# Sharing the first and last 32 score columns of five query tiles, written by matmuls in 32x64 tiles of the array

## The chip, the cores and the metric

The kernel runs on one core of one Trainium2 chip. The metric is the device time of one execution in microseconds (us), and a kernel's time is the median of its runs. Besides the timed runs there is one profiled execution, from which every busy time, start and duration below is taken. The engines are TensorE (PE, with its weight loads as PEld), VectorE (DVE), ScalarE (ACT), GpSimd (POOL) and SyncE (SP, which issues most DMAs).

## The reference

The input x has 2048 rows of 512. Four layers are added to it one after another, each on the layer norm of what stands before it: linear attention (A), attention in a sliding window (B), and both once more with the same weights. There are 32 heads of 16 columns.

```python
def _B_ref(x, wqkv, wo):
    H = 32; Dh = D // H; W = 256
    ...
    scores = jnp.einsum("bhqd,bhkd->bhqk", q, k) * (Dh ** -0.5)
    idx = jnp.arange(S)
    mask = (idx[:, None] - idx[None, :] >= 0) & (idx[:, None] - idx[None, :] < W)
    scores = jnp.where(mask[None, None], scores, -1e9)
    p = _softmax(scores, axis=-1)
    o = jnp.einsum("bhqk,bhkd->bhqd", p, v)
    ...
x = x + _A_ref(_layernorm(x), A_wqkv, A_wo)
x = x + _B_ref(_layernorm(x), B_wqkv, B_wo)
x = x + _A_ref(_layernorm(x), A_wqkv, A_wo)
x = x + _B_ref(_layernorm(x), B_wqkv, B_wo)
```

A query sees itself and the 255 rows before it. Turned round, a key at row n is seen by the queries n to n + 255, and a block of 64 keys by 320 queries.

## The kernel before, in words

The rows are cut into 16 tiles of 128 (j = 0 to 15; the title of the change counts from one, so its tiles ten to fourteen are j = 9 to 13). The layers overlap: `middle(2)` runs the second layer (window) tile by tile, with the keys of the third layer behind it; `middle(3)` runs the last layer (window), with the outputs of the third ahead of it. For each tile, `middle` calls `front` three tiles ahead (`a_out`: the third layer's output product; `norm`: layer norm and transpose to xT; `b_qkv`: the queries into XQ, the keys by way of a DMA into kB), `b_v` one tile ahead, then the scores, the values and the output product of the tile itself.

**Scores.** kB holds keys so that one weight load of 32 rows serves two heads: 32 rows are two heads of 16 columns, and the 128 columns of the weights are 64 keys times two heads, laid out key by key (block diagonal by a DMA that writes zeros between). Four row groups of the array (gq, 32 rows each) work on four pairs of heads at once, each into a PSUM bank of its own. So the scores stand transposed: 128 partitions are 64 keys times two heads, and the free side is the queries. Partitions 0 to 63 are the first 32 keys of the block, 64 to 127 the last 32.

`b_scores` (matmuls L634, exps L644, masks L652) writes, for one half-tile b of 64 keys and two of the four groups f, the first 256 of the block's 320 query columns: 8 matmuls of 256 columns, two exps on ACT of 1024 elements per partition (two banks each) into the buffer of probabilities P, and on DVE one mask of the first 64 columns (upper triangle). There are four such bursts to a tile, so eight exps. `b_far` (L723, L732) writes the last 64 columns of all of a tile's blocks at once: 32 matmuls of 64 columns and two exps of 1024, into columns 256 to 319 of P; `far_masks` (L703 on POOL or L704 on DVE) zeroes the lower triangle there. The far columns are read by the values of tile j + 2, the others by those of j to j + 2. P is a ring of four slots in the last layer, three in the buffer pb and one in vp; tiles 3, 7, 11 and 15 use vp.

`b_values` (L753) multiplies P by the values, 24 matmuls of 34 columns for a group f; the 34 columns hold two heads' 16 values and a one for the sum; DVE divides (L765, L766). `b_out` transposes by DMA (L371), multiplies by wo (L400) and adds (L568).

**Packed tiles.** `middle` holds a second form for tiles named in PACK: before `b_scores` it calls `b_edge`, and in place of `b_far` only `far_masks`. In `b_scores` the window then begins 32 queries later (sh = 32): it covers columns 32 to 287, and its mask has 32 columns in place of 64. The two strips that are left, columns 0 to 31 and 288 to 319, each matter for one half of the partitions only: no query of the first strip sees the last 32 keys of its block, and no query of the last strip sees the first 32. `b_edge` puts both in one strip: partitions 0 to 63 hold the first strip's scores, 64 to 127 the last one's. Two exps of 512 elements write it to columns 288 to 319 of P, and a DVE operation named `ma` copies partitions 0 to 63 from there, times the triangle, to columns 0 to 31. Then `far_masks` zeroes what must be zero at 256 to 319. The values of tile j read what `ma` writes. Partitions 64 to 127 of columns 0 to 31 keep the zeros that the mask of the slot's earlier tile left. PACK is empty in this kernel, so no tile takes this form.

**Order.** Nothing is scheduled at run time. `Plan` builds a list of operations with their dependencies and a key; `place` reads from TABLE (a compressed string) one order of all operations, the engine of each operation that has a choice, and a PSUM bank for each tile of PSUM. Each engine runs its operations in that order, and `synchronise` adds the semaphore waits. The costs given with each operation (`occ`, `act`, `dve`) belong to the planner and have no effect on the running program.

Of the kernel before, what the change touches and what calls it, by code (L numbers as in the profile page):

```python
# [217 lines left out]
PACK = {}  # L218
# [5 lines left out]
def bass_view(x, free):  # L224

    return bass.AP(x.tensor, x.offset, [x.ap[0]] + free)


class Plan:
# [430 lines left out]
    def b_edge(self, j, key):  # L660
# [224 lines left out]
    r"q*|$7s?a*Wo~3T8S1PT(rNZdAdWFiZPN~}}oerXQtJ5mI-lf87)baEk6;9t(XH*7Fy0I#tU#pC|pk_T=WzuKW9Cc3_{YJ&tqKByjx`2AChN~v3rY@-7sS)bF",
    r"s-;J&@cO+fq$B9kYLxn@N~nlBvo5TQ=t%m5imbEfggUEsDv{2ntxl}7>nJ*jE~=C2LaLZ{y0}iJE2|PZs!py;>Iy1{4z5b+e5$rCtb(bEx{l7N>*?XTk}j>A",
    r">&m){uA)|{7P_jgrbp=Nx`uA4SF5_Zl4_;bsHVD|ZmgT>J*u2)qZ{fby1s6$%d5Srfj+0!sz$o4KCddOeQKm$r$*`h>VlfBtE<s^j=rc4=`p&b`lPC=HF~U`",
    r"s}JjO`m>s+$Lj}bf_|tDsEK;MKBC*}NqT`^t1qdAdYWFOzo_YYonEXTsmZ#7e&c57y?TmXuV?Cxx|9B@rs`RGgWjh*>y7%d-mkmp<$9BTtXAmFdWn9bw&<05",
    r"ss5&}=w-UA4gy#8QGG)Pg=_kj?xu^uDt$~BhhT71AJ+%;6CFgK&`<SAy;YZhQ+k_zrh~%{9aJCG+x2t3Q<sEb`nrChcj?tSD!kOuAOr;0r644n)*<vOeMX0Z",
    r"(hwT%=;&}(hk<jthPtQE>xb@wzN@?IG7t}X=!^OkB!JVfN0)`_@LI=*a&QJ>K@GUAW5WoD2{mCP#DV*|HY9_D@J7GYF(5fS(C_p^Jqj-A6gmZ@)Q|LT9T&>O",  # L890
    r"d!0%@)~TQZeATISY8VY+Asmc>G>}G*g$NKHB0@zN2X$aPoP|U%0qQ~}hy;nD9-M=ox)!v6^N<88LsDo37hon_gjtXhT0&a*rY}Ji_^xL|1NfoSK_f^HKlN>B",
    r"2(96R&HxJP!ySkW8b0ZaFcI!Tc9;YJA9Wj;440uDTmgi}Ku|`1(QTouz6zNj3Y62Ibq>e^)gUJ{fvS)TGDB0C2hAWG<c2A*0H#8D&5#G?Lj|1|3^a#mS|A@R",
    r"ghh}QrolB>4A&t)SSSGPA-cW+OP~Wd=m;_NQdk9@Af{dhYhVt<(#v5kbcWT?ORs>Quo8Ofb+7^Y>4H!Q`s(!%2K(r+xE2b-6W9o^-7_cxn;;x+hNAEk!s7?1",
    r"h#%oORKhK=6?(xZsEoVe0Yt#wPz4`CM9ii8z<tQABjF?H3teCu&VZ_zM@Pon*bg2<6zm3Zu|MS1(=ng!3IiY>R>OgC2WQ|Qh>z9r4b;Fr&>h~wUbqK$u?O_m",
    r"@1Q2`gKaQCZ-*B!9bUp`*a5fTJ?w{McoV)r3OoR>;42)2*RTtc<4jD1QE{M7g5Mw-?u73!7@{L$VjKeLa3~ytx|k5tV+<Syvv4@X#MzhuQ(`8ZgGsR-X2w)l",
    r"A5&u%jD^kdFtos|SPPFpMy!o#uqCF&)>sD#+aO~ryocGaEgJj**)a~z#h=g!6JQQ(j5$%EU}roEO|T0tN5E!y47#Gm6__8pqs8OU4qv#H*dBZ0JiL!5paVX@",
    r"lh6YluEE&Y5er}t?1byEAojwC_|gT%ZnzeM;Rbw!y|EB(#6Gwln_^*n<u>7C%!Ng;FD}BO*bj5#V%&@ku^7(B;+O}Q;0`Q-3vd^{!G-u1^WjcxfP-{!9IS_6",
    r"UVMikaF~AULgF4AqE}-A+KZvEBo5W3a36-ogw!8P<4|0R1F#GZ!$h<SpWr|&i_7pSCZ;3!47cELJc?U!HzuJGcnp)$S8Ph#a6cxa@7Rn+Vsd(p%_#*9#&7rn",
    r"4`2&=iKFl%wxl0;5I^H~9F41J5FWx$xS9^*7(~iQt!OMVWun%UlG+f_8v1~#C=GqV%ybeB39Y5nbR5%?rJwj7(~+WA=;#EtrEH|>6awX-(>M;Z(-|C(K`0kZ",
    r"z_S>Xa??Z%M(1!6p2s|tlZsJRx`4syJ%ymxSb{##I?78OX+2%U;`EU&VIkT;ou~-qqmq<`I#YfsOyQ_E6`*!hkor(jYEPx8FLj{)^odH-0P07Vu?!8QD_E93",  # L900
    r"Q%KrKS1|((qVN=oBG5IgOxLj+g{JNlk#^H2ibOqVG=-%-G?pUMWK2(cX$nT6F;tGCQWg3_(WnAdrRWrfwox^jirc9?^`zmngTB&W>PjQ2It`&NG>%5lX8J}$",
    r"={p^u8dQmD(iS>I!zc!ArCt=1YSBSDLbYiW)u9`Blq%9q98b6K7)_v9bb%()aWZ_7CXw(A(tL?51IMN_beZbXSvpMh2zei!pmP+5_R~qKPv<EppQ0-ij89Vo",
    r"x=IZxIEQ4%*JvhPr%)V%XVG2yL9;0|N8}*<ljcw)&cbs^aaNv3k$E!Br$)4s7SI%GOxbuB-J>Qnl@`){ipmctE=A*M6pvc)LyFEf=n=K#=|p^s9@8U^Pt1?`",
    r"Cbi-xbeI=W7=FS}DK5w0BOH&P@@)#sQ8+#?rlTB=pYamP%i%dD=jRB#lw$ER%Evi5JKv$@l#8EHY+gYH_!zIG+<b;}@L4X(=lDDq=Qw<U^Kc?A#uvFHALr6s",
# [36 lines left out]
class Kernel(Plan):  # L941
# [152 lines left out]
```

## Time and profile before

| | |
|---|---|
| Median of 3 runs | 416.91 us (416.87 to 417.95) |
| The profiled execution | 415.97 us |
| Its span | 414.2 us |
| Mean granted clock of TensorE | 0.999 |
| Busy: PE, DVE, ACT, POOL | 387.9, 346.8, 345.8, 117.7 us |
| Weight loads (beside PE) | 258.5 us |
| Exps of the wide scores, L644, both window layers | 224, 206.7 us |
| Exps of the far columns, L732, with 1024 elements, into pb | 50, 49.6 us |
| Share of the chain that ended last | PE 48%, ACT 35%, DVE 9%, DMA 5% |

A busy time counts the time in which an engine has an instruction in flight; two that overlap count once. The mean duration of one instruction is therefore longer than busy time over count where instructions follow each other closely. "<-" names what ended an engine's idle time. The chain of work that ended last is followed back from the last instruction, at each step to what released it. Numbers behind an L are lines of the kernel before.

### The profile page before, as it was taken

How to read it: one execution, taken by the hardware profiler on the slowest of the kernel's cores; microseconds unless marked ns; L12 is line 12 of the kernel's file. 1: busy time of each engine (PE TensorE's matmuls, PEld its weight loads, DVE VectorE, ACT ScalarE, POOL GpSimd, SP SyncE). 2: the span in 40 equal slices, each digit the busy share in tenths (PEclk: the TensorE clock that was granted, in tenths of full speed). 3: DMA queues.
4: the chain of work that ended last, by engine and by line, in shares of the span. 5: the costliest groups of instructions: out<-in, count | busy, mean ns of one | idle time of the engine just before them, and what ended most of it. 6: DMA issues, size and time to landing. Idle time of an engine off the chain costs nothing.

```text
span 414.2 us, 17130 instructions
## 1 busy us (share of the span) xinstructions
PE 387.9 (94%) x7481; PEld 258.5 (62%) x7555; DVE 346.8 (84%) x803; ACT 345.8 (83%) x432; POOL 117.7 (28%) x211
## 2 busy tenths in 40 slices
PE   7999999999999999999999999999999989988886
PEld 3545676766575577565666777586757745556554
DVE  5997898989989988778978689989799687776575
ACT  2624449998999999999997245999999999999992
POOL 4784833111241243230112302220132215230111
PEclk9999999999999999999999999999999999999999
DMA  7545316632233624444213100353306623273361
GB/s 246 177 79 148 104 40 119 131 92 68 64 96 78 110 73 113 80 107 106 56 29 69 26 2 27 93 148 79 81 7 134 137 56 95 60 159 96 93 121 54
DMA packets 67555, 37.83 MB, mean 91 GB/s; under 512 B 48248, under 2 KB 62584, under 8 KB 67480
## 3 DMA queue, kind: packets, MB, share of 16 engines
q1 hardware_dynamic: 67040, 35.54, 36.7%
q8 instruction: 60, 0.98, 1.0%
q0 software_dynamic: 432, 1.18, 0.9%
q14 instruction: 15, 0.12, 0.1%
q10 hardware_dynamic: 8, 0.00, 0.0%
HBM read 6.29 MB, written 2.10 MB: 20 GB/s over the span
## 4 chain that ended last, share of the span: by engine, by line
PE 48%; ACT 35%; DVE 9%; DMA 5%; issue 2%; SPq 1%
ACT pb L644 22%; PE ps L400 17%; PE ps L414 13%; PE ps L753 7%; ACT pb L732 6%; ACT vp L644 5%; PE ps L634 5%; PE ps L475 2%; DMA XQ<-xn 2%; DVE stats L361 2%; DMA xres<-in_A_x_dram 2%; DVE xres L568 1%; DVE XQ L557 1%; PE ps L723 1%; ACT vp L732 1%
## 5 line engine op out<-in xcount | busy, mean ns | idle before, releaser
L644 ACT ACTIVATE pb<-ps 128x1024 bf16<-128x1024 f32 (+2 forms) x224 | 206.7, 1042 | 4.5 <-PE ps L634 3.7
L753 PEld LDWEIGHTS ps<-vB,pb 128*128 128x128 bf16 x2560 | 77.5, 96 | 11.7 <-issue 4.6
L753 PE MATMUL ps<-vB,pb 128*128 128x34 bf16 x2560 | 83.2, 177 | 1.1 <-ACT pb L644 0.6
L414 PE MATMUL ps<-xT,wBp 128*128 128x128 bf16 x1024 | 69.2, 219 | 1.2 <-DVE vp L586 0.5
L414 PEld LDWEIGHTS ps<-xT,wBp 128*128 128x128 bf16 x1024 | 59.2, 98 | 13.6 <-issue 4.4
L423 ACT ACTIVATE tE<-ps 128x512 bf16<-128x512 f32 x64 | 38.5, 612 | 34.3 <-PE ps L400 15.5
L363 POOL TENSOR_SCALAR ve<-mv 128x1 f32<-128x1 f32 x64 | 16.7, 261 | 172.6 <-DVE mv L362 170.5
L634 PE MATMUL ps<-XQ,kB 32*128 32x256 bf16 (+2 forms) x1024 | 49.6, 267 | 5.0 <-ACT vp L644 1.4
L732 ACT ACTIVATE pb<-ps 128x1024 bf16<-128x1024 f32 x50 | 49.6, 1066 | 0.4 <-PE ps L723 0.2
L568 DVE TENSOR_TENSOR xres<-ps,xres 128x512 bf16<-128x512 f32 x63 | 43.1, 685 | 7.6 <-PE ps L400 7.0
L400 PE MATMUL ps<-wA,XQ 128*128 128x512 bf16 x176 | 46.2, 379 | 2.7 <-issue 0.6
L652 DVE TENSOR_TENSOR pb<-pb,tri 128x512 bf16<-128x512 bf16 x112 | 44.7, 412 | 4.0 <-ACT pb L644 3.7
L703 POOL TENSOR_SCALAR_AFFINE_SELECT pb<-pb 128x1024 bf16<-128x1024 bf16 x26 | 29.8, 1148 | 62.9 <-DVE pb L652 32.6
L361 DVE BATCH_NORM_STATS2 stats<-xres 128x6 f32<-128x512 bf16 x64 | 43.6, 686 | 2.6 <-DMA xres<-in_A_x_dram 1.8
L364 POOL TENSOR_TENSOR rs<-ve,negh 128x1 f32<-128x1 f32 x64 | 37.8, 591 | 5.3
L634 PEld LDWEIGHTS ps<-XQ,kB 32*128 32x128 bf16 x1024 | 15.5, 92 | 33.6 <-ACT pb L644 9.2
L414 PE MATMUL ps<-XQ,wA 128*128 128x128 bf16 x512 | 34.7, 219 | 0.3 <-DVE o L766 0.3
L414 PEld LDWEIGHTS ps<-XQ,wA 128*128 128x128 bf16 x512 | 30.4, 98 | 5.7 <-DVE o L766 0.6
L400 PE MATMUL ps<-wBv,xT 128*128 128x512 bf16 x112 | 31.5, 380 | 2.2 <-issue 1.3
L400 PE MATMUL ps<-wBo,oT 128*128 128x512 bf16 x105 | 28.8, 380 | 4.2 <-issue 1.1
L400 PE MATMUL ps<-M,XQ 128*128 128x512 bf16 x112 | 30.7, 380 | 2.1 <-issue 1.0
L765 DVE RECIPROCAL rc<-ps 128x16 f32<-128x16 f32 x64 | 16.1, 252 | 19.3 <-PE ps L753 19.0
(110 smaller groups left out, 532.8 us busy)
## 6 DMA issues: line engine op xcount, KB each, us to landing
vB<-vS SPq DMA_DIRECT2D x64, 136.0 KB, 2.6
kB<-vp SPq DMA_DIRECT2D x64, 128.0 KB, 2.7
wA<-in_A_wqkv_dram SPq DMA_DIRECT2D x3, 512.0 KB, 4.6
out_dram<-xres POOLq DMA_DIRECT2D x9, 128.0 KB, 2.8
xres<-in_A_x_dram SPq DMA_DIRECT2D x2, 512.0 KB, 4.3
pb<-in_B_wqkv_dram SPq DMA_DIRECT2D x1, 1024.0 KB, 5.6
xres<-in_A_x_dram SPq DMA_DIRECT2D x3, 256.0 KB, 4.8
out_dram<-xres SPq DMA_DIRECT2D x6, 128.0 KB, 2.4
```

The costliest lines, as they stand in the source:

```text
L361: self.on("DVE", "stats", lambda e: e.bn_stats(K.stats[:, t, :], K.xres[:, t, :]), key, dve(512), rd=[("xres", t)], wr=[("stats", t)])
L364: self.pow = self.on("POOL", "pow", lambda e: e.tensor_tensor(K.rs[:, t, :], K.ve[:, t, :], K.negh[:], ALU.pow), key + 0.03, (640, 690), r ...
L400: m = e.matmul(K.ps(ps), lhs(c), rhs(c), start=c == 0, stop=c == 3)
L414: m = e.matmul(K.ps(ps)[:, f * P:(f + 1) * P], w(c, f), xT(c), start=c == 0, stop=c == 3)
L423: self.on("ACT", "E", lambda e: e.activation(K.tE[:, s, :], K.ps(ps), ACT.Exp, bias=0.0), key, act(512), wr=[("tE", s)], ps=[ps])
L568: self.on("DVE", "res", lambda e: e.tensor_tensor(K.xres[:, t, :], K.ps(po), K.xres[:, t, :], ALU.add), key, dve(512), rd=[("xres", t)], w ...
L634: m = e.matmul(K.ps(ps[gq])[:, ns * i:ns * i + ns], K.kB[rows, j % 4, 2 * f + b, :, :], K.XQ[rows, f, q:q + ns], start=True, stop=True, ti ...
L644: return e.activation(out(2 * h, 2, ns), i, ACT.Exp, bias=0.0, scale=0.25)
L652: return e.tensor_tensor(x, x, K.tri[:, 0, sh:64].unsqueeze(1).unsqueeze(1).to_broadcast([P, 4, n, 64 - sh]), ALU.mult)
L703: return e.affine_select(out=x, in_=x, compare_op=ALU.is_ge, fill=0.0, base=-2, pattern=[[0, 16], [-2, 64]], channel_multiplier=1)
L732: return e.activation(far(h), i, ACT.Exp, bias=0.0, scale=0.25)
L753: m = e.matmul(K.ps(ps)[:, 34 * u:34 * u + 34], K.P((b // 2) % rp)[:, gq, f, o:o + P], K.vB[:, (b // 2) % 4, b % 2, r, :], start=i == 0, s ...
```

## The change

PACK names tiles 9 to 13 of the last layer (phase 3). `b_edge` is rewritten: each matmul of 128 weight columns and 2 x 32 queries becomes two of 64 weight columns and 32 queries, at array positions of 32 rows by 64 columns. Half u = 0 takes the first 32 keys with the first strip's queries and writes partitions 0 to 63; u = 1 takes the last 32 keys with the last strip's queries (288 further on) and writes partitions 64 to 127 of the same PSUM columns. The two DVE copies (`gc`) that the old form of `b_edge` needed to bring the strips together are gone, and the exps read 32 columns in a row where they read 32 of every 64. TABLE is replaced as a whole, since the list of operations is another.

```diff
-PACK = {}
+PACK = {3: (9, 10, 11, 12, 13, )}
...
             for f in range(4):
                 for b in range(2):
-                    q = P * j + 64 * b
                     for gq in range(4):
                         rows = slice(32 * gq, 32 * gq + 32)
-                        c = 128 * f + 64 * b
-                        m = e.matmul(K.ps(ps[gq])[:, c:c + 64], K.kB[rows, j % 4, 2 * f + b, :, :], bass_view(K.XQ[rows, f, q:q + 32], [[288, 2], [1, 32]]), start=True, stop=True, tile_position=(32 * gq, 0))
+                        c = 64 * f + 32 * b
+                        for u in range(2):
+                            q = P * j + 64 * b + 288 * u
+                            half = slice(64 * u, 64 * u + 64)
+                            m = e.matmul(K.PS[half, ps[gq].banks[0], c:c + 32], K.kB[rows, j % 4, 2 * f + b, 32 * u:32 * u + 32, :], K.XQ[rows, f, q:q + 32], start=True, stop=True, tile_position=(32 * gq, 64 * u))
             return m
 
-        self.pe("s", put, key, 1, 512, mode=(32, 128), occ=245, rd=[("kB", j % 4, 0), ("kB", j % 4, 1), ("XQ", j), ("XQ", j + 2)], ps=ps)
+        self.pe("s", put, key, 1, 256, mode=(32, 64), occ=540, rd=[("kB", j % 4, 0), ("kB", j % 4, 1), ("XQ", j), ("XQ", j + 2)], ps=ps)
...
-            side = lambda c, two=two: bass_view(K.PS[64:128, two[0].banks[0], c:c + 32], [[512 * (two[1].banks[0] - two[0].banks[0]), 2], [64, 8], [1, 32]])
-            self.on("DVE", "gc", lambda e, side=side: e.tensor_copy(side(0), side(32)), key, dve(512), ps=two)
 
             def ex(e, h=h, two=two):
-                return e.activation(edge(h), K.pair(two, [[128, 4], [64, 2], [1, 32]]), ACT.Exp, bias=0.0, scale=0.25)
+                return e.activation(edge(h), K.pair(two, [[64, 4], [32, 2], [1, 32]]), ACT.Exp, bias=0.0, scale=0.25)
...
 TABLE = (
...
 )
```

More of the change, by code (lines that the diff above doesn't have):

```diff
@@ L885 @@
[L885 to L892, printed above, removed]
@@ new lines @@
+    r")71&(R0!CiPO2FyBwSai;f4wYITS%$xT#93nMy-wxTQ|1FmPM#RHs!MXs8$(sd(^G<x{Vef$A_zy;ix@U6mHzs5?ratf~QT)etpQ<%M(*7K*6cDj$S{^pGDi",
+    r"z<U)Q-l+mGOqEmxAwEQaoT?C5hzNO90vN6wj8F+7h>8S>AR`1)iJ_8;44I&cDh!#S2xNhpP!zI4ew7rGKrzS;1ypg!1|^}qss)vx1Qb+tpdvJd@=yU*sH&<N",
+    r"RE8>06)LN0&>U8(+E84zfK{rDY78x*AvA$qYPD(&b)gYdP-j#<SflF0SyfIofHtsOol~t~I1Gh7Y6KjBy=o-Pgjp~O4#I4>r#`6BuuqMFRWJwctFiD=jf3-Q",
+    r"Jj{hdFb~?o1h}A9!vi%RroaODq}ISxSO~*lBD8~Pup1`9ba<%R!&>M7lVJwzfld%qEroUPNG*f)a1pw|a@YWiU?c2>#n2Hp!6jG%ogoljhQm+<_rW#ztggTj",
@@ new lines @@
+    r"_@V;i4LAx#aX$pXV-N_g!&NATk03BSf#VPqH^T|o0>v>1Y=g%T47b7x*bc!lG6sc}Py%<rO$dR{AQ+UyDEJ(9!AS^-r7$Xn!c*`9Zoz3d19#vhoQ0>*6>h^h",
+    r"h=bkW0-V5jcoKI)X{?HI@f4Q97<d<|VN4u`)iD|l$5?n8&qES?1tTyzzJ_F&4C3QGcmv5HDZYiW7#m08eMkW*@Bx&=lz0Xo!dVQBDd97O!BkL9rNVF+7Q<tC",
+    r"9EG*;97e#=SOIHe4NQPzuqGzNu~-MsV>29w$+03P!WNhqr(<fIft9d1et`=(6Td<|{029%0p7yzkOu2xT}+F&@g1bY@%RDK;{<GoSyACdd=C>5uoYfH#5PD+",
+    r"3N&8E($E?|LI%u+pCA%u#OzoZ8(}8QfmN_E=ER6t2IgQEY=V<;E;hx<SQauPV>y_I26N#Qi~@qWaRGJ*i&t<F=E1fY74l+B%!gNTAv$b_^YI$C$Hf>8R$vEQ",
@@ new lines @@
+    r"f*o-c&cf)h6k|YlT#4`9GVB4%@tx}lvvCdfhIN=93*c&8i@hKe^?}e-5Fg=sEQC*R0~W@O7=|9>I}A(Z={;7UO&E?gV-E~ZAFv|r#CsTlo?=hDkCi9~^uj6h",
+    r"0CPe_>W!T+66J!M^bkAaRO*Adp)ba!JkSN>P(PeTx2Q73rB~P=yW#-cg|Bfp-llHY7vA6=oQ7NQBi_JgScSIYTkHpS@HtkcZ8#N^&|dt6$*3BA#(nq#tJ8jb",
+    r"iAiZYCZOpQneJjDnn6+M3(lm0cpalsLVDw7QG6PN$>}Smp?EYH6H{$UOGHC38V$uASclS428vD@DFq$C7?hGSQC(_Esi+1W#AcM54q;8oOq$YDbE-uxiK!K}",
+    r"pe$slHGM;&tn?i%H6TaXs3B!1MS*BG<)x0)hz?_Cx<g9|C>9;TyVQx=&@zfi_Xw#gHKC*U+AXL1)Rwx_96E;W=s0$xRrG-JQG0qwYp4h1rw-JGR?|A_4}qyC",
@@ new lines @@
+    r"6`&xro_bM1`rtOuT53!=s5dR3Lez)qQBEpM3uz;*pt)3p7EvzRM)RmB6{8*Wit^BWdQIDD0IZ~-l$!>^8yZBxXb`-0!D$x_fp~fk)u#{?Uk`@jw3|Xw2}+>*",
+    r"Qb`(2{iqZ@qJ;V}^{3J_gc9jPG?WtSO>~%^P!heF_R<mBNuOy8HP%V>S8AdMQZoINw$c|mO3$dN-bagR7(J)=)J*TEkJMbR(C_E~4W|#ZQXixd^pd_2=~X(F",
+    r"9!X0`>lXSLrPjwOxn@0zK2dtTTBpzhXfzouI;GB_t^Q7LX^qaP*J`DmPNQ4uEE@C)YNfMj)UEYN3Z%zSR(*=b(hE9GIrKORtaIu!G@gR!vowKn>2<n@4yv>3",
+    r"w>p?UN5%9zeV*Fu-1-8&*F|*)T|jr#d2}XSNPp0Ib!J^$7t~>NPyJEn)1P!3onQCTg>_r~S(ni5bZ^~Pm(>0AMJlB)QGZ=p_tC-idL33@rgXZC4ymtDMIBCG",
@@ new lines @@
+    r"rLH=J4zG9W4SJW3pu6eNdZdo1C(>>`TBp^MXn^jaBk4+dl%7o8br~I5SJvfp6x~U0(V=t|9aV4DWp!0OR1eg{b!S~oZ`0NFApJ!T(>3%yJy>tlL-YZ?N!Qf1",
+    r"bTnOFZ`S*DbUi{J(qHv88lw;EgZesE&|~!xeS^m782X&vqsME*6ZCm~R0~hjz!$V-<e2)DCO)Rm=vaEMuB|WX)4Gm6uIuWvIxwHmmvj(5sq5*>y1ov|!TE}w",
+    r"uCMA49E@k^+xnZHsY7yj4#eN}EFFO}vE$iVab}*QBl1K&S2xf*^gKODH`G~pyS}3v>B)M&zN;hiJsn#|;i)<l$I;C=Dqqw0b#rFEt|RdSexNnC;DbCx-_Q>^",
+    r"u3n%Y@k1S(AM+uO!;kbW9hwhwTwbW3a2Srpi*#;|&Wm+k4$I*<1~1Whc&X0HG5N91&awE3UZ!(!K0d|Eb$mX;IXN2_=F^;ji*hbL%V+qeKF3A4IG^XET$1zi",
@@ new lines @@
+    r"F)qL*I3Bm>f?SNBatAKO&$tkG<kp;!+i)T-&55}!m*FJ*oO^RwE<=5|6Ti~sxE=T9vQ&j%@N4~&%TafJqg!!j?!ig9AGhQ#oQ!+&Ois>Ebqao_XK`0f$-Q_s",
+    r"ALnlTT$kq;x<6OoIs8(e;EG(82k=R*%u{(FzvAgUh^z559?a>v5?AM?{GOL_4PMT#xh5~<6<muy@M5098F&%b<{|usm+(;j$aOdsXXLuPl0We<Ud6+CF0bZ!",
+    r"yoMX|d>+B6`7JNtk=%sS@LC?l7q}^><%>L;FY!7a!|(VqujkLaf$Q-`uFqgLaRZ*jo4Fxh;VpcXukltM%iA~|U+3CpGB@JwJdUSu9dm<sFq)lA<|dElU3`lt",
+    r"@NVA66L~-H;oH2I5AYqn%i7#yHuw1pXEYhiSI%X=aW<3NWHQ-J4r5GC^PRJpJVu$UCa)2b&tx`%jWq>LU6bF`GeJy!)7}I%&U7#hOjy&=%rFhjOjE!#GT}@o",
@@ new lines @@
+    r"Gte|PgG>|C*#t99O(4_7gfPuaNE6(2HLc8G6W+8o-Ao}f#B?{!O<~i+v@mVVWHZ!6Ftf}s6Uy{4ZB0uP(eyRLO*=Ei6fynG2ou^AHM7lBGtvw&Jxy^l%JeeR",
+    r"Oc*oT^f$dtF*C+YH@i#;GuB)%yG==R(S(poW{(LebIdvuO6HnzX1y72=9&4Xfb2CJ%mQ=S>@x*rg4u6Ynk%M|tTI>40rSjkG}p{Sv)a5c3r%QQYZjU3CX7rn",
+    r"o6L1nSRR=hX0ushipXOV$rP0>CbC&<o|s~?)P$AdGSNga$ILPlPS%*{=7foAVwjg^xw&b=%W?D6Y&Ew`G!sE$npftwxno|NSmv%dXjYimCZ@bGCrvE5XG)pa",
+    r"^2wAohfEy#Yz~`<a>T@yZRV)?Vz!$H=9}4J-kM1A-Rv~)Ok_E25*j66O(OH&l#s+Go_sJ-<fBO-NlZmaYNASf0WlIyDoHJ4<&23TmF27vIc4sfL~_ocB$k9i",
@@ new lines @@
+    r"Qc|=e5tdX^N&-t787ZY@l%$rVQcaxnkQy>tdP*QkCcUJ(q?6u~T+&M)DI+PQuauRPl0o`OHt8=xq?}}zpc2QFmtc}Z;+g@HR%%H`iDzm`CaEp)O>{|MGD{t4",
+    r"Bv~Z2$tq2xuB0)!rHn~y%9_S9L@JspGE~x;s#3uuGsC2UBsb+uGf836n>^B7@=8-lX$DGp(?SMGDziZbOFkJV8)bqVludF-#!E|SCx@k#<dWgiUN%c>86h2H",
+    r"i%gVBvQ^s13u!Bp<)v(s?NU!($qtz!l}sm@C6!HmnJqabfo&jjq@f&>*OJh7mg7>xCbBi{R2d^DWS-2GX);#cNMid|=F4=cW#7pjSs+!+dpRXD<b!mSnX*^T",
+    r"$WGZOyX3Silx4D87Rd^!Z5PXOxg<wriFA>ra#^~{Y606#uE;e>Vvh*gvy#-_kdLxo$bOP!_JEv}>+(fDi?LtD+M9At>e%GAu3af9tk^*Is?@XRC9pkjZpj7t",
@@ L934 @@
+    r"?G#WnfBXAx`;5FoOF)hNxBMf}S7{1(M!_Eis{jLEpb`M(lLs_1k^JaB|HI_xKzq-L@}6Cv#MkwnqyGXk!96+",
 )
```

65 lines of the change are left out of this document (20 added, 45 removed).

## The prediction

> **What bounds the kernel now.** I read the page first, then the busy time by stages, then the chain of work that ended last, and last the groups of the final stage with shapes kept apart. The slices of the page:
>
> ```profile
> PE   7999999999999999999999999999999989988886
> DVE  5997898989989988778978689989799687776575
> ACT  2624449998999999999997245999999999999992
> ```
>
> The profile cuts the span of 414.2 us into 40 equal slices. ScalarE (ACT) is at 9 without a break only in the last third. PE is at 9 nearly everywhere, but falls to 8 in the last slices, where ACT is full. The same in us, for the stretch in which the last layer begins, for that which holds its tiles nine to fourteen, and for the tail (columns: length, then busy time of PE, weight loads, DVE, ACT, POOL, each with its count of instructions, then clock and DMA):
>
> ```profile
> 280.00:338.00 58.00, 55.51 (x1279) 38.86 (x1290) 48.22 (x109) 56.71 (x64) 12.46 (x17) 1.00 0.37 79
> 338.00:400.00 62.00, 54.46 (x1275) 34.91 (x1282) 45.40 (x105) 62.00 (x69) 14.52 (x21) 1.00 0.44 103
> 400.00:414.20 14.20, 9.66 (x249) 7.01 (x250) 8.53 (x22) 6.55 (x13) 1.95 (x4) 0.98 0.29 80
> ```
>
> From 338 to 400 us ACT is busy for 62.00 of 62.00 us, while PE idles 62 - 54.46 = 7.5 us and DVE 16.6 us. The granted clock is 1.00, so no throttle enters the sum. The chain of work that ended last says that these ACT instructions are the end's own path (columns: start, length, engine, output, line, count):
>
> ```profile
> 346.97 12.84 ACT pb L644 x14
> 359.80 1.83 ACT pb L732 x2
> 361.63 5.50 ACT pb L644 x6
> 367.13 1.83 ACT pb L732 x2
> 368.97 7.33 ACT vp L644 x8
> ```
>
> One exp of 1024 elements per partition holds ACT for 12.84/14 = 0.917 us, whether it is of the wide scores (L644) or of the far columns (L732). ACT works tile by tile through its queue: counting eight L644 and two L732 for each tile, tiles nine to thirteen (counted from 0; the ten to fourteen of the title) begin at about 350 us, and the last far exp (tile thirteen) ends at 399.7. So every exp that the change touches lies in the stretch where ACT alone sets the time. After 400 us comes a tail of 14.2 us (last values, their transposes, the output product), which the change leaves as it is.
>
> **The change part by part. Removed: half of ten exps.** In each of the five tiles the two L732 exps of 128x1024 go, and two of 128x512 come. For 1024 elements I have 0.917 us; for 512 the last stage holds one row, that of tile fifteen (from 0):
>
> ```profile
> L644 ACT ACTIVATE pb<-ps 128x1024 bf16<-128x1024 f32 x68 | 64.0, 1108 | 0.0
> L644 ACT ACTIVATE vp<-ps 128x512 bf16<-128x512 f32 x4 | 2.1, 594 | 0.1
> L732 ACT ACTIVATE pb<-ps 128x1024 bf16<-128x1024 f32 x16 | 16.0, 1082 | 0.0
> ```
>
> Busy time over count gives 2.1/4 = 0.525 us for 512. The saving is 0.917 - 0.525 = 0.39 us at least; the mean durations give 1108 - 594 = 0.51 us at most (durations overlap their neighbours). I take 0.42, near the first, which is time held and not latency. 2 x 5 x 0.42 = **4.2 us off ACT** (3.9 to 5.1), all of it on the path. The input now goes in pieces of 32 columns where L732 goes in pieces of 64 and L644 in 256; both old forms take 0.917 us, so I put the pieces at nothing.
>
> **Added: the burst on PE.** The far burst goes and the edge burst comes, 64 matmuls of 32 columns for 32 of 64. The old burst and the only column-tiled work of the kernel (first two rows, in layer 3's end):
>
> ```profile
> 243.75 0.27 PEld L537 LDWEIGHTS ps<-XQ,zs 128*32 128x32 bf16 x16
> 243.81 0.40 PE L537 MATMUL ps<-XQ,zs 128*32 128x128 bf16 x16
> ...
> 344.27 0.29 PEld L723 LDWEIGHTS ps<-XQ,kB 32*128 32x128 bf16 x32 [0.87 <-ACT vp L644]
> 344.27 0.41 PE L723 MATMUL ps<-XQ,kB 32*128 32x64 bf16 x32 [0.38 <-ACT vp L644]
> ```
>
> The last of the 32 starts 0.41 - 0.19 (its own duration) = 0.22 us after the first: 7 ns for each, and in the single records four row groups start within 9 ns and the next four 20 ns later, 29 ns a round, 8 rounds, 0.23 us. From below, the new burst is 8 rounds of eight matmuls at the same 29 ns: nothing is added. Nearer is the far burst's mean, 7 ns a matmul: 64 x 7.3 = 0.47 us, **0.24 us more a tile, 1.2 us in all**. From above: one after another at the pace of the values' matmuls (L753; 34 columns, 25 ns apart): 64 x 25.3 = 1.62 us, 1.39 more a tile, 7.0 in all. I take the middle one, since the column tiles of L537 do run beside each other: 16 matmuls of 128 columns start within 0.40 - 0.22 = 0.18 us, 12 ns apart, where 128 columns at full width (L414) take 56. The Trainium skill ("TensorEngine Tiling (Array Packing)", Instruction Overhead) speaks against the change here: a matmul costs some 60 cycles however few columns it has, so one should not split a dimension that is already short. The trace agrees in that 34 columns take 25 ns and a round of 64 takes 29, so that 32 columns win next to nothing; by that rule alone, with the tiles side by side, the burst would take 8 x 25 = 0.20 us, an estimate, and with them in a row the upper bound above.
>
> The burst is covered by PE's 7.5 us of idle time in this stretch, which has to hold both the 4.2 us by which the stretch shrinks and the 1.2 us: 5.4, leaving 2.1. That is little, so ACT will not stay at 100%. The row 280 to 338 shows what happens when PE is that full: PE 55.51/58 = 95.7%, ACT 56.71/58 = 97.8%. At 97.8% the 62.0 - 4.2 = 57.8 us of ACT work take 59.1. So **1.3 us come back as waits of ACT for PE**.
>
> **DVE.** Each tile's four diagonal masks (L652) fall from 512 to 256 elements: two in a row take 0.75 us, so about 0.33 each at 512, and something between 0.17 and 0.33 at 256; I take 0.21, 0.5 us less a tile. One new mask of 1024 on 64 partitions (ma, L689) comes, nearest row L704 at 0.69: 0.2 us more a tile, 1 us over five, in DVE's 16.6 us of idle time. Without that cover it costs 1 us. The copies gc that the diff deletes were never issued, as PACK was empty: nothing. POOL keeps its masks or hands them to DVE at 0.69 each; both have room.
>
> **Moved.** In a packed tile the first half's wide scores start 32 queries later and reach into x-tile j+2 (before: j+1), and the edge burst is needed by the tile's own values, where the far burst was needed only two tiles on. The first wants the queries of tile j+2 one score burst earlier, 1.8 us (two exps). The last queries are copied to XQ (L389) at 381.2 and tile thirteen's scores come at 384.6; the transpose of those rows was issued at 369.0 and their projection began only at 377.0, so there is room to bring it forward. No DMA is added, and SP's and POOL's queues get no more issues. Then nothing is late. The second is the rival below.
>
> **The orders.** The diff replaces the whole table of order, engines and banks, and as text it shows nothing of what stands where. I put it at nothing, with 3.4 us to either side, 1% of the 338 us ahead of these tiles. That is a judgement, not a row.
>
> **Sum** against the profiled execution (415.97 us, of which 414.2 is span and 1.8 lies around it): - 4.2 + 1.3 = -2.9, so 413.1. The median of the runs is 416.91, 0.94 above that execution; the forecast for a median is 416.9 - 2.9 = **414.0 us**.
>
> **Rivals.** (1) **The new mask's wait.** PE takes its queue in order, and the values (L753) of tile j now stand behind burst, two exps, ma. If the edge comes last in its tile, that is 0.34 + 2 x 0.5 + 0.2 + 0.7 = 2.2 us before the values and all that stands behind them (next scores, and so ACT). Five times 2.2 less 4.2 is +6.8 at worst: 423.7. It decides from 4.2/5 = 0.84 us a tile. Against it: the plan's keys put the edge ahead of the eight wide exps, 7.3 us of cover, though the table has the last word; and DVE waits for exps only some 2 us between 324 and 400, so it masks soon after them. 12 in 100, half of it close to no change.
> (2) **The burst is slow.** By the upper bound, PE works 54.46 + 7.0 = 61.4 us; at 95.7% that is 64.2, 2.2 longer than now: 419.1. It decides from (0.957 x 62 - 54.46)/5 = 0.97 us more a tile. L537 speaks against it. 8 in 100.
> (3) **Loads of one row group wait.** Neighbours in the new burst share a row group. If the second's load (93 ns) waited until the first's matmul (188 ns) is through, a row group's eight such pairs take 8 x 0.28 = 2.2 us, 2.0 more a tile, and (54.46 + 10)/0.957 = 67.4: 422.3. The Trainium skill ("TensorE: Matmul & The Clock Gate", The mechanism) says that loads overlap running matmuls only in another row group. The four column tiles of L537 share all their rows and start 12 ns apart with loads of 97 ns, which is against it: 3 in 100.
> (4) **The order costs elsewhere.** 3.4 us or more lost ahead of 338 us, where PE's digit is 9 and any wait of it shows: 414.0 + 3.4 = 417.4; it decides from 2.9 (10 slower, 4 no change). That it gains there, 410 to 412: 5 in 100.
> My forecast, 412 to 415.6: 58 in 100.
>
> **The numbers.** About 0.3%, 1.25 us, is what a measurement here can tell from none. Faster: 58 + 5 = 63. Within: 6 + 4 = 10. Slower: 6 + 8 + 3 + 10 = 27. The range goes from 411.0 (5.1 saved on ACT, and a little from the order) to 420.5 (the slow burst and what the order may add); it leaves out the waiting loads and the worst of the first and fourth rival.
>
> **What would show it.** Right: ten exps of 128x512 in b_edge that hold ACT about 0.5 us each; ACT above 97% in the stretch of the five tiles, which is some 3 us shorter; the burst's 64 matmuls starting within 0.5 us; the tail still 14 us. Wrong: the values waiting for DVE's ma (rival 1), starts in the burst 25 ns or more apart (2 and 3), or a last layer that begins later than now (4). If PE kept ACT full after all, the 1.3 us would not come back and the time would be 412.7.

## The result, and the profile after

The changed kernel takes 421.5 us (median of 20 runs, 418.49 to 424.23), the kernel before 416.94 in 20 runs on the same chips: ratio 1.0111, 95% interval 1.0091 to 1.013. The change makes the kernel **slower by 4.6 us**; 2.9 us faster was forecast. The profiled execution took 424.05 us, span 422.3, near the upper end of the runs, so terms are taken from its trace and the sizes of effects from medians. Below, medians are of all runs of a kernel and ratios of the fast ones alone, where a run more than 1.5% above the fastest of its kernel counts as slow.

The page's slices (each a fortieth of the span):

```profile
PE   8999999999999899989998999999999979899866
DVE  5997899999989899879776699988898787676763
ACT  2633559998999999989995246999999999899970
PEclk9999999999999999999999999999999999899996
```

ACT is still at 9 in the last third, but its last slices are now 7 and 0, and the clock (PEclk) dips in the slice from 359 to 370 us and at the end. The three stretches shown of before, with the tail to its new end (length, busy time of PE, weight loads, DVE, ACT, POOL with counts, then clock and DMA):

```profile
280.00:338.00 58.00, 55.70 (x1270) 39.87 (x1280) 48.36 (x110) 57.01 (x65) 12.57 (x18) 1.00 0.34 84
338.00:400.00 62.00, 54.26 (x1419) 36.34 (x1421) 44.93 (x104) 58.32 (x68) 14.99 (x21) 0.97 0.35 89
400.00:422.30 22.30, 15.39 (x352) 10.49 (x351) 12.58 (x32) 10.25 (x17) 2.77 (x4) 0.81 0.37 96
```

From 338 to 400 us ACT was full before; now it idles 3.7 us. Over the whole span ACT is busy 341.4 us where it was 345.8: the 4.4 us were saved, and the time grew. Three lines of ACT's timeline (start, busy, line, output, count, and in brackets the idle time before them and what ended it) show a saved exp and two new waits:

```profile
364.75 1.08 ACT L685 ACTIVATE pb<-ps 128x512 bf16<-128x512 f32 x2 [0.36 <-PE ps L676]
367.56 5.91 ACT L644 ACTIVATE pb<-ps 128x1024 bf16<-128x1024 f32 x6 [1.72 <-PE ps L634]
413.25 0.66 ACT L644 ACTIVATE vp<-ps 128x256 bf16<-128x256 f32 x2 [3.23 <-PE ps L634]
```

Two edge exps hold ACT for 1.08 us in place of 1.83. Behind them ACT waits 1.72 us for the next score burst, and 3.23 us in the tail. What PE did (same columns):

```profile
181.21 0.81 PE L400 MATMUL ps<-wA,XQ 128*128 128x512 bf16 x3 [0.98 <-DMA XQ<-xn]
232.28 1.24 PE L400 MATMUL ps<-wA,XQ 128*128 128x512 bf16 x5 [1.63 <-DMA XQ<-xn]
363.99 0.68 PE L676 MATMUL ps<-XQ,kB 32*64 32x32 bf16 x64
366.35 0.61 PE L414 MATMUL ps<-xT,wBp 128*128 128x128 bf16 x4 [1.35 <-issue]
411.49 1.49 PE L400 MATMUL ps<-wBo,oT 128*128 128x512 bf16 x3 [2.60 <-DMA oT<-o]
```

The first two lines lie in the middle layers, which the change does not speak of: there PE now waits 2.6 us for transposes by DMA. In the trace of before the same two took 0.21 us (at 185.8 us) and nothing. The other lines are the edge burst, a stop of 1.35 us for which the profile shows no reason, and a wait in the tail, where a transpose landed 5.4 us after its issue.

I matched each DVE and ACT operation of one trace with itself in the other and subtracted the starts. At 163 us the changed kernel is some 0.7 us behind, at 191 us 1.4, at 233 us 2.7, at tile nine's first exps 3.6, at tile fifteen's 4.0, and at the end 8.2. So most of what is lost ahead of the tail is lost **before the first packed tile**. That made the first theory: the orders cost the time, and packing in itself gains. The rival: packing itself costs it, by the cover that the halved exps no longer give to PE.

### The profile page after: what moved, and what is told of

Read it like the earlier page. It is cut to its first block, busy times and chain, and to the rows that moved or that the text cites. A ratio compares the mean times of both kernels' runs of the same rounds, so it can differ in the third digit from the quotient of the medians.

```text
span 422.3 us, 17462 instructions
## 1 busy us (share of the span) xinstructions
PE 391.1 (93%) x7641; PEld 261.5 (62%) x7715; DVE 348.1 (82%) x803; ACT 341.4 (81%) x429; POOL 125.8 (30%) x218
## 4 chain that ended last, share of the span: by engine, by line
PE 51%; DVE 21%; ACT 14%; DMA 7%; issue 3%; POOL 3%; SPq 0%; DVEq 0%; POOLq 0%
PE ps L400 17%; PE ps L414 13%; PE ps L753 10%; ACT pb L644 9%; PE ps L634 5%; DVE stats L361 3%; DMA XQ<-xn 3%; DVE pb L652 2%; DVE XQ L557 2%; DVE xres L568 2%; ACT vp L644 2%; PE ps L475 2%; DMA oT<-o 2%; DVE xn L365 1%; POOL rs L364 1%
## 5 line engine op out<-in xcount | busy, mean ns | idle before, releaser
L414 PE MATMUL ps<-xT,wBp 128*128 128x128 bf16 x1024 | 69.7, 220 | 2.8 <-issue 1.8
L414 PEld LDWEIGHTS ps<-xT,wBp 128*128 128x128 bf16 x1024 | 59.4, 98 | 16.1 <-issue 7.0
L703 POOL TENSOR_SCALAR_AFFINE_SELECT pb<-pb 128x1024 bf16<-128x1024 bf16 x34 | 38.9, 1145 | 84.0 <-DVE pb L652 28.7
L363 POOL TENSOR_SCALAR ve<-mv 128x1 f32<-128x1 f32 x64 | 15.6, 243 | 156.2 <-DVE mv L362 153.9
L400 PE MATMUL ps<-wA,XQ 128*128 128x512 bf16 x175 | 46.7, 379 | 4.4 <-DMA XQ<-xn 2.6
L652 DVE TENSOR_TENSOR pb<-pb,tri 128x512 bf16<-128x512 bf16 (+1 forms) x112 | 46.0, 421 | 4.8 <-ACT pb L644 4.5
L568 DVE TENSOR_TENSOR xres<-ps,xres 128x512 bf16<-128x512 f32 x63 | 43.0, 685 | 7.5 <-PE ps L400 6.8
L732 ACT ACTIVATE pb<-ps 128x1024 bf16<-128x1024 f32 x42 | 41.3, 1053 | 1.0 <-PE ps L723 0.8
L400 PE MATMUL ps<-wBo,oT 128*128 128x512 bf16 x107 | 30.7, 392 | 6.5 <-DMA oT<-o 2.6
L414 PE MATMUL ps<-XQ,wA 128*128 128x128 bf16 x512 | 36.0, 219 | 0.0
L414 PEld LDWEIGHTS ps<-XQ,wA 128*128 128x128 bf16 x512 | 30.5, 98 | 6.4 <-DVE XQ L425 0.6
L400 PE MATMUL ps<-wBv,xT 128*128 128x512 bf16 x111 | 31.2, 380 | 1.6 <-issue 0.8
L400 PE MATMUL ps<-M,XQ 128*128 128x512 bf16 x114 | 30.2, 380 | 2.3 <-issue 1.1
L644 ACT ACTIVATE vp<-ps 128x1024 bf16<-128x1024 f32 (+2 forms) x32 | 26.8, 917 | 5.2 <-PE ps L634 5.1
```

The lines of the kernel that those rows point to most:

```text
L400: m = e.matmul(K.ps(ps), lhs(c), rhs(c), start=c == 0, stop=c == 3)
L414: m = e.matmul(K.ps(ps)[:, f * P:(f + 1) * P], w(c, f), xT(c), start=c == 0, stop=c == 3)
L568: self.on("DVE", "res", lambda e: e.tensor_tensor(K.xres[:, t, :], K.ps(po), K.xres[:, t, :], ALU.add), key, dve(512), rd=[("xres", t)], w ...
L644: return e.activation(out(2 * h, 2, ns), i, ACT.Exp, bias=0.0, scale=0.25)
L652: return e.tensor_tensor(x, x, K.tri[:, 0, sh:64].unsqueeze(1).unsqueeze(1).to_broadcast([P, 4, n, 64 - sh]), ALU.mult)
L703: return e.affine_select(out=x, in_=x, compare_op=ALU.is_ge, fill=0.0, base=-2, pattern=[[0, 16], [-2, 64]], channel_multiplier=1)
```

## Experiments

TABLE is data, so I exchanged parts of it between the two kernels: up to a given operation in the order, on the engines and in the banks of the one, from there on as the other. Operation 1,080 is at about 163 us, 1,560 at 244 us, 2,088 at 328 us, ahead of tile eight's scores. In the diffs "..." in TABLE stands for that order; the short diffs show PACK alone, and each of these kernels carries its own TABLE and the new `b_edge` as well. Each run stands against runs of the kernel before that were taken along with it, so the time of before differs a little from one comparison to the next. All kernels compute the whole reference.

### The orders without packing, and packing without the orders

**after_order_plain**: the changed kernel's order, nothing packed.

```diff
-PACK = {3: (9, 10, 11, 12, 13, )}
+PACK = {}
```

> The changed kernel's order, engines and banks, but no tile packed: the far columns' burst and its two exps of 1024 stand where the edge burst and its exps stood, and ma is gone. Theory A (the order made anew costs, the packing gains): 421.5 plus the 2.9 us that the packing was to save, 421 to 425. Rival B (the packing itself costs: its burst, its mask's wait, more PE instructions): back at the time of before, 416 to 418.

423.18 us in 4 runs, before 417.32; ratio 1.0127 (1.0075 to 1.018). The orders alone cost some 6 us (5.9 by medians). That packing gains on top of them is not shown by this run: 1.7 us by the medians (423.18 - 421.5), but 0.7 by the ratios (1.0127 and 1.0111), within their intervals.

**before_order_three**: the order of before, tiles 9, 10 and 11 packed in place.

```diff
-PACK = {}
+PACK = {3: (9, 10, 11)}
```

> The order, engines and banks of before, with tiles 9, 10 and 11 packed in place: the edge burst stands where the far burst stood, ma right behind its exps on DVE, nothing else is moved. Theory A: three fifths of the saving, 416.9 - 1.7 to 416.9 - 2.5, 414.4 to 415.2. Rival B: three fifths of the loss of 4.6, about 419.7.

419.61 us in 10 runs; ratio 1.0057 (1.003 to 1.0084). The rival had this right: packing in the old order loses. ACT's timeline, behind tile nine's edge, and PE's twelve us later:

```profile
360.20 1.09 ACT L685 ACTIVATE pb<-ps 128x512 bf16<-128x512 f32 x2
362.11 3.81 ACT L644 ACTIVATE pb<-ps 128x1024 bf16<-128x1024 f32 x4 [0.82 <-PE ps L634]
```

```profile
373.64 0.59 PE L400 MATMUL ps<-wBo,oT 128*128 128x512 bf16 x2 [1.85 <-DMA oT<-o]
```

The 0.74 us saved at the edge (1.83 - 1.09) come back as 0.82 of waiting. PE starts the next score burst at 361.66, 2.22 us after the edge burst, and has no idle time between: values and 16 matmuls of L414 stand there in its order. The far exps, 1.83 us, covered nearly all of that; 1.09 us do not. Later PE, in its fixed order, stands 1.85 us for a transpose that landed 5.9 us after its issue (median of its kind 2.5); ACT waits 1.73 us for that.

**before_order_five**: all five packed; the bursts of tiles 13 and 14 had to be rearranged by hand, and nine PSUM tiles change banks.

```diff
-PACK = {}
+PACK = {3: (9, 10, 11, 12, 13)}
```

> The order of before with all five tiles packed. In tiles 12 and 13 the edge has to come ahead of the tile's own values, so the bursts of tile 13 and two of tile 14 change places with the far bursts, and the values of tile 13 stand a little later; nine PSUM tiles change banks. Theory A: 413 to 414.5. Rival B: about 421.5.

429.42 us in 4 runs; ratio 1.0281 (1.0231 to 1.0331). Both missed. From 380 us to its last scores ACT waits some 10 us for PE, about 0.5 us at most pairs of exps and twice over 2: this rearrangement was bad, and the run says little on packing.

**after_order_tail**: the changed kernel with tile thirteen's output product placed behind the last score burst in PE's order, so that the burst need not stand behind the late transpose.

```diff
 TABLE = (
...
 )
```

> The changed kernel, with one thing moved: on PE the output product of tile 13, which waits for its transposed rows from a DMA, stands behind the last score burst and the first half of the values of tile 15 and not ahead of them. If the tail's loss is PE standing at that DMA (2.6 us in the profile, with the clock halved behind it): 417.5 to 419.5. If the tail is only late because what comes ahead of it is late: 421 to 422.

424.35 us in 4 runs; ratio 1.0167 (1.0128 to 1.0207). Missed: no gain. In its trace the tail does lose less (starts 7.4 us behind at tile fifteen's exps, 8.1 at the end, where the changed kernel went from 4.0 to 8.2), but the part ahead, whose order is the changed kernel's own, is already 5.6 us behind at 262 us where that was 2.6. Part of it is the clock: behind the second of the two waits above it is halved in this trace, six L400 matmuls take 2.74 us, and the lag grows by 3 us there; in the changed kernel's trace the clock stays at 1.00 behind the same wait, and the lag grows by 1.5. One trace of this kernel thus does not size a term.

### Halves exchanged

**early_before_late_after** and **early_after_late_before**: cut at operation 2,088.

```diff
 TABLE = (
...
 )
```

> The first 2,088 operations stand in the order, on the engines and in the banks of the kernel before (all of the last layer up to tile 8's first scores), the rest as in the changed kernel, packed tiles and tail included. Theory (the remade order loses some 3.3 us ahead of the packed tiles, by the starts of matched exps in the two traces): 421.5 - 3.3 = 418.2 us, 417.5 to 419. Rival (the order ahead costs nothing that lasts; all of the loss is made in the packed tiles and the tail): 421 to 422.

> The mirror image: the first 2,088 operations as in the changed kernel, the rest as in the kernel before, no tile packed. Theory (the early part of the remade order costs 3.3 us by itself): 416.9 + 3.3 = 420.2 us, 419.5 to 421. Rival (it costs nothing that lasts): 416.5 to 417.5.

The first takes 416.71 us (12 runs; ratio 0.9992, 0.9973 to 1.001), the second 421.33 (6 runs; 1.0103, 1.0078 to 1.0128), before 416.69. So **the order ahead of tile eight carries the whole loss**, 4.6 us, more than the 3.3 of both my expectations, and both times fall just outside the ranges expected; the packed tiles and the tail as the change has them cost nothing together.

**early_before_late_plain**: the first of the two with nothing packed.

```diff
-PACK = {3: (9, 10, 11, 12, 13, )}
+PACK = {}
```

> The order of the kernel before for the first 2,088 operations, of the changed kernel after them, and no tile packed: far bursts and ten exps of 1024 in the places of the edge bursts and their exps. Compared with the same order with five tiles packed (416.7 us): if packing keeps the whole 4.2 us on ACT less the burst's 1.2 (first theory), 419.7 us or more; if it keeps about 1 us (in the trace of the packed kernel tile 15's exps stand 0.9 us earlier against the kernel before than tile 9's), 417.3 to 418.5; if it keeps nothing, 416.4 to 417.

418.6 us in 12 runs, before 416.81; ratio 1.0033 (1.0008 to 1.0058). That is just above the middle one of the three ranges. Packing is worth 418.6 - 416.7 = 1.9 us in the late order; by the ratios (1.0033 and 0.9992) it is 1.7, and their intervals taken together leave some 1.3 us to either side. The late order costs about as much (418.6 - 416.81 = 1.8). ACT's waits for PE from 345 to 402 us (who waited, for what: us, times, longest), packed and then plain:

```profile
ACT pb L644 <- PE ps L634: 1.0, 1, 1.0
ACT vp L644 <- PE ps L634: 0.6, 1, 0.6
ACT pb L685 <- PE ps L676: 0.4, 1, 0.4
```

```profile
ACT vp L644 <- PE ps L634: 1.0, 1, 1.0
```

In this order one of the five edges (tile ten's) has a wait before and behind it, 0.35 + 0.98 us, which is more than its exps save; PE stood 1.15 us for the banks that these exps hold before it could start the burst that ACT waits for.

**early_before_late_four**: the same order, tile ten left plain.

```diff
-PACK = {3: (9, 10, 11, 12, 13, )}
+PACK = {3: (9, 11, 12, 13)}
```

> As the kernel with the early order of before and the late order of after, but tile 10 stays plain; tiles 9, 11, 12 and 13 are packed. In the trace of the kernel with five, ACT waited 0.35 us for tile 10's edge burst and 0.98 us for the score burst behind it, more than the 0.84 us that its shorter exps save; at the other four edges no such wait stands behind the exps. Cover theory: 0.5 us less than 416.7, so 415.9 to 416.5, the fastest of all. Rival (each packed tile is worth the same): 416.7 plus the fifth part of what packing is worth in this order, 416.8 to 417.5.

415.63 us in 12 runs; ratio 0.9976 (0.9951 to 1.0001). This is the lowest median of all, 1.2 us below before, but the interval just reaches no change. It lies below the cover theory's range, and further from the rival's; against the order with five packed tiles (0.9992) the ratios differ by 0.7 us, with some 1.3 to either side, so that leaving out tile ten gains is not shown by the time. The trace bears the mechanism out: from 345 to 402 us ACT waits once for PE, 0.6 us, where it waited 2.0 in all with five.

### Where ahead of the packed tiles

The order of after up to a cut, then that of before; and single stretches of it, in each direction; nothing packed but in the third.

```diff
 TABLE = (
...
 )
```

> The changed kernel's order for its first 1,080 operations (up to about 163 us, tile 9's scores of the middle layer), then the order of the kernel before, no tile packed. Theory (the early order loses its time in steps along the whole way, by the starts of matched operations some 1.2 us by there): 417.6 to 418.6 us. Rival (one place at the end of the middle layer, 227 to 233 us, makes the loss): 416.5 to 417.2.

> The same with the cut at operation 1,560 (about 244 us, behind the middle layer's end). Theory (steps along the way, 3.1 us by there): 419.5 to 420.5 us. Rival (the loss is made in the last layer's early tiles, 244 to 335 us): 416.5 to 418.

> The changed kernel, five tiles packed, with operations 1,080 to 1,560 (about 163 to 244 us, the second half of the middle layer) put back into the order, on the engines and in the banks of the kernel before. Theory (PE's two waits for the transposes XQ<-xn at 181 and 232 us, 0.98 and 1.63 us in the changed kernel's trace and 0.21 and none in the other's, and what hangs on them, are made by the order of this stretch): 421.5 - 3.4 = 418.1 us, 417.3 to 418.8, and both waits gone. Rival (what stands ahead of the stretch or behind it makes the loss): 420.5 to 422.

> The mirror image: the kernel before, no tile packed, with only operations 1,080 to 1,560 in the changed kernel's order. Theory: 416.8 + 3.4 = 420.2 us, 419.4 to 421, with the two waits for XQ<-xn in its trace. Rival (the stretch loses only together with the order ahead of it): 416.5 to 417.5.

> The kernel before with only operations 1,080 to 1,380 (about 163 to 212 us) in the changed kernel's order: of the two waits the first alone. Theory (each wait costs about what it lasts): 416.8 + 0.8 = 417.6 us, 417.0 to 418.2. Rival (the whole loss begins here): 419.5 or more.

> The kernel before with only operations 1,380 to 1,560 (about 212 to 244 us) in the changed kernel's order: of the two waits the second alone. Theory (each wait costs about what it lasts, and this one 1.2 to 1.6 us): 418.0 to 418.8. Rival (the second wait comes only of what the first has shifted): 416.5 to 417.2.

| kernel | us (runs) | ratio to before, interval | PE's waits for XQ<-xn near 180 to 187 and 231 to 232 us |
|---|---|---|---|
| after_to_163us | 416.79 (12) | 0.9998 (0.9974 to 1.0022) | 0.48, none |
| after_to_244us | 420.18 (6) | 1.0076 (1.0046 to 1.0106) | 0.86, 1.50 |
| after_but_163_to_244us | 418.34 (12) | 1.0042 (1.0016 to 1.0067) | 0.60, 0.19 |
| only_163_to_244us | 419.1 (6) | 1.0061 (1.004 to 1.0083) | 0.71, 1.46 |
| only_163_to_212us | 417.72 (12) | 1.0028 (1.001 to 1.0047) | 0.89, none |
| only_212_to_244us | 418.84 (8) | 1.0047 (1.0029 to 1.0066) | 0.65, 1.49 |

Up to 163 us the order costs nothing (my expectation of steps along the whole way missed there). The stretch from 163 to 244 us costs 3.4 us behind the changed early part, 2.5 by itself, and the changed kernel without it loses 1.8 us against its before and not 4.6. Of the other five, only_163_to_244us falls 0.3 us below its theory's range and only_212_to_244us 0.04 above. Each half costs something, the second more (1.1 and 2.2 us). The second wait follows its half: above a microsecond at 232 us wherever that half is the changed one, at most 0.19 where it is not. The first wait does so less clearly: in the table it lasts 0.71 to 0.89 us where the first half is the changed one, but also 0.48 to 0.65 where it is not, as in after_to_163us, which loses nothing. The starts of DVE's residual additions (L568) show that the time is lost at the second wait and stays lost: in only_163_to_244us they are 1.5 us behind those of before at 227 us, 3.0 at 233, and 2.9 at the end. What makes the second wait is read from DVE's timeline in only_212_to_244us and then in before:

```profile
223.64 0.69 DVE L568 TENSOR_TENSOR xres<-ps,xres 128x512 bf16<-128x512 f32 x1 [0.49 <-PE ps L400]
226.59 0.43 DVE L652 TENSOR_TENSOR pb<-pb,tri 128x512 bf16<-128x512 bf16 x1 [0.68 <-ACT pb L644]
226.94 0.41 DVE L365 TENSOR_SCALAR xn<-xres,mv,rs 128x512 bf16<-128x512 bf16 x1
```

```profile
222.75 0.69 DVE L568 TENSOR_TENSOR xres<-ps,xres 128x512 bf16<-128x512 f32 x1 [0.32 <-PE ps L400]
226.07 0.41 DVE L365 TENSOR_SCALAR xn<-xres,mv,rs 128x512 bf16<-128x512 bf16 x1
226.39 0.42 DVE L652 TENSOR_TENSOR pb<-pb,tri 128x512 bf16<-128x512 bf16 x1
```

Tile thirteen's rows are finished by the second layer (L568), normed (L365) and sent by DMA into XQ, where the third layer's projection (L400) waits for them. In the new order the output product that L568 adds comes 0.9 us later. Half of that, 0.48 us, PE was already late at 207 us, ahead of the changed stretch, behind a longer first wait (0.65 us for 0.21); the rest is work that now stands ahead of the product in PE's queue. A mask that waits 0.68 us for ACT stands ahead of the norm in DVE's, but from L568 to the norm it is 3.3 us in both traces, so the mask adds nothing. The transpose, some 4.2 us under way in both, is issued at 227.37 and not 226.50. And PE's order behind the values' burst (96 matmuls), first in only_212_to_244us, then in before:

```profile
227.54 2.56 PE L753 MATMUL ps<-vB,pb 128*128 128x34 bf16 x96
231.59 1.47 PE L400 MATMUL ps<-wA,XQ 128*128 128x512 bf16 x6 [1.49 <-DMA XQ<-xn]
```

```profile
226.67 2.56 PE L753 MATMUL ps<-vB,pb 128*128 128x34 bf16 x96
229.30 0.81 PE L400 MATMUL ps<-wA,XQ 128*128 128x512 bf16 x3
229.94 0.39 PE L451 MATMUL ps<-vp 128*128 128x128 bf16 x4
230.73 0.61 PE L400 MATMUL ps<-wA,XQ 128*128 128x512 bf16 x2
```

In before, PE has 1.4 us of work behind that burst that needs no transpose, and reaches tile thirteen's rows at 230.73, as they land. In the new order that work is done elsewhere, and PE stands. The exchanges show that this stretch, its order with its engines and banks, makes the second wait and the loss. How much of it the later product makes, and how much the work that no longer stands behind the burst, was not tried one by one.

### Cover

**before_order_one**: tile nine alone packed in the order of before.

```diff
-PACK = {}
+PACK = {3: (9, )}
```

> The order of the kernel before, with tile 9 alone packed, its edge burst in the place of its far burst. Cover theory (the two shorter exps save 0.84 us on ACT, and ACT then waits some 0.8 us for the score burst behind them, since 0.54 us of exp no longer covers PE's refill): no change, 416.5 to 417.4. Rival (what a packed tile shifts runs into the transposes that come by DMA, as with three tiles): 418 to 420. If the burst were free and the saving kept: 416.1.

418.98 us in 12 runs; ratio 1.0043 (1.0018 to 1.0068). The wait is there (0.81 us behind the edge, as in the trace of three), and the starts are 0.5 us further behind from there on. But in this trace most of the loss, 3.3 of 4.4 us at the end, is made in the tail, as the rival had it, if by another transpose. The chain of its last part, and that of before:

```profile
407.14 4.22 DMA oT<-o
```

```profile
406.07 2.40 DMA oT<-o
```

The tail's order is that of before, the transpose takes 1.8 us longer, and behind PE's stand of 2.05 us the clock is halved and the last six matmuls take 1.72 us of the chain, not 0.88. Its runs go from 416.09 to 421.21, so this varies between executions of one kernel; why the transpose is late in this one is not shown.

**before_order_three_double**: as three tiles, with each edge exp done once more into columns that nobody reads.

```diff
             def ex(e, h=h, two=two):
+                e.activation(bass_view(K.P(sl)[:, 2 * h, 0, 320:352], [[2816, 2], [704, 4], [32, 2], [1, 32]]), K.pair(two, [[64, 4], [32, 2], [1, 32]]), ACT.Exp, bias=0.0, scale=0.25)
                 return e.activation(edge(h), K.pair(two, [[64, 4], [32, 2], [1, 32]]), ACT.Exp, bias=0.0, scale=0.25)
```

> As the kernel before with tiles 9, 10 and 11 packed in place, but every exp of an edge burst is followed by a second one of the same 512 columns whose result nobody reads, so that ACT works 1.08 us where the far exp took 0.92 (six exps). Cover theory (what was lost in three packed tiles is PE's refill no longer hidden, and what that shifts): 417 to 418.6, faster than the 419.6 us of three packed tiles although ACT does more. Rival (the burst itself and what it does to PE costs the time): 419.6 plus up to 3.2 us, so 420 to 422.8.

421.82 us in 6 runs; ratio 1.0125 (1.0095 to 1.0155): 2.2 us more than single exps, for 3.2 us more work. The expectation of the cover theory fell, and its mechanism did not: with 2.07 us of exps at the edge, ACT has no wait directly behind any of the three edges. The time goes to two other waits, of which PE's timeline shows the first:

```profile
362.63 0.27 PE L754 MATMUL ps<-vB,pb 128*128 128x34 bf16 x4 [0.99 <-DVE pb L692]
```

L692 here is `ma`: the later exps delay it, and tile nine's values stand 0.99 us for it, the wait of the prediction's rival 1. Later PE stands 2.27 us for DVE's copy of keys (L586), and ACT 2.40 for PE. So in this order an edge has to be short for the values and long to cover PE's way to the next burst, as far as these two traces show it.

## Why the prediction was wrong, point by point

- **The orders** is the step that failed: "I put it at nothing, with 3.4 us to either side". They cost 5.9 us by after_order_plain (423.18 against 417.32). By pieces it is nothing up to 163 us, 3.4 from there to 244, some 1.1 from there to 328 (420.18 to 421.33, within the runs' spread) and 1.8 behind. Nothing of this was read from a row, though a sign of it was there: the waits for XQ<-xn sit where, in the trace of before, a transpose lands just as PE comes to it, and the table can be decoded to see what moves there.
- **Rival 4**, that the order costs elsewhere, was the right mechanism. Its price began at 3.4 us and would have decided from 2.9; what it measured ahead of the packed tiles is 4.6. It had 14 in 100, which was too little.
- **ACT's saving**, 4.2 us, was right: 0.54 us an exp, 4.4 us less of ACT over the span.
- **1.3 us come back** was probably too low. Packing is worth 1.9 us by medians in the late order and not 2.9, so about 2.3 of 4.2 come back, though with noise of 1.3 us to either side 2.9 is not excluded. The reason given, PE too full in the mean, was not the one seen: single waits at single edges, 1.33 us at tile ten alone in the late order, none at the other four. What takes the rest was not found.
- **The burst**, 0.24 us more, was right: 0.68 us in place of 0.41. With its last matmul's own 0.196 us off, 64 matmuls start within 0.49 us, 8 ns apart. Rivals 2 and 3 fell. The Trainium skill ("TensorE: Matmul & The Clock Gate", The mechanism) says that loads overlap running matmuls only in another row group; here two matmuls in a row share a row group, and by their records each loads for 101 ns, each runs for some 190 (the profile models a matmul's end), and they start 8 ns apart in the mean, so the trace does not bear that out for two column tiles.
- **Rival 1** fell: nobody waits for ma in the changed kernel's trace. **DVE** hid its work.
- **Moved** was right as far as seen: no packed tile waits for queries.
- **The tail**, "which the change leaves as it is", was wrong as to its order, since TABLE is new there too. "Still 14 us" held in early_before_late_after (its last additions start 0.04 us off those of before) and not in the changed kernel's profiled execution, where one transpose lands 5.4 us after issue and the clock is halved for 6.8 us.

What stays open: the stop of 1.35 us ("issue") at 365 us, behind tile ten's edge burst. It is in the traces of all three kernels with the changed order up to 163 us, packed tiles and the changed late order (1.35, 1.61 and 1.55 us, each amid the same eight L414 matmuls), and not in early_before_late_after, which has the same edge and late order behind the early order of before. There PE stands 1.15 us for banks right behind the same matmuls, and ACT waits 0.98 us and not 1.72 for the next scores, so the stop and the slower clock behind it cost ACT some 0.7 us. A fetch of 16 KB of instructions by DMA starts just ahead of the stop (363.69 us in the changed kernel), but one starts at the same place (360.94 us) in early_before_late_after. Nothing in a trace says what PE lacked.

## What to carry to other kernels

When a change comes with a schedule made anew, the schedule is the change: exchange stretches of the two schedules before pricing the edit. Look in the old trace for transfers that land just as their reader arrives, since any reordering there becomes a wait of an engine that runs in order. A shorter operation gains only as far as the engine that feeds it gets to the next piece sooner: look at what stands in that engine's order between the two.

## What the runs showed of the hardware

- **A transpose by DMA** took 2.4 us from issue to landing in one execution and 4.2 in another with the same order around it, and up to 5.9 among other transfers. In early_before_late_four a load of keys made PE wait 1.68 us at 82 us, where before, with the same order up to there, had no wait:

```profile
82.57 0.40 PE L634 MATMUL ps<-XQ,kB 32*128 32x256 bf16 x8 [1.68 <-DMA kB<-vp]
```

- **The clock** of PE halves for 3.4 us, or twice that, behind a stretch in which PE was less busy, but not behind every such stretch. In the changed kernel (same columns as the stretches above):

```profile
229.60:233.00 3.40, 1.77 (x46) 1.42 (x44) 1.80 (x7) 0.00 (x0) 0.79 (x2) 1.00 0.06 13
362.70:366.10 3.40, 2.29 (x116) 2.06 (x116) 2.27 (x6) 2.78 (x4) 0.00 (x0) 1.00 0.23 53
366.10:369.60 3.50, 3.25 (x70) 2.20 (x71) 1.57 (x6) 1.96 (x3) 0.79 (x2) 0.51 0.36 75
```

  From 362.7 us PE was busy 2.29 of 3.40 us, and the next 3.5 us had the clock at 0.51. The Trainium skill ("TensorE: Matmul & The Clock Gate", What's actually happening) says that the clock halves after an idle window of about 3.4 us. The length of 3.4 us agrees; idle the window was not, its longest stop is one of 1.35 us. But from 229.6 us, a window 39 such lengths earlier in the same trace, 1.77 busy us of 3.40, with a wait of 1.63, left the clock at 1.00. So the busy time of a window alone does not decide, and no run here shows what does. The changed kernel's runs with a mean clock of 0.994 and more took 418.5 to 422.1 us, those with 0.992 and less 421.8 to 424.2.
